# One contraction block of the third query/key piece moved ahead of the second memory rows, with a third staging buffer

## The chip, the cores and the metric

The kernel runs on one core of one Trainium2 chip. The metric is the device time of one execution in microseconds (us), lower is better. TensorE is called PE, its weight loads PEld, VectorE DVE, ScalarE ACT, GpSimd POOL. A ratio in the batches is the mean time of one kernel's fast runs over that of the kernel before in the same rounds, with the first round, in which the profile is taken, left out. So it is not quite the ratio of the medians and means that stand beside it, which keep that run. A "batch" is a set of kernels timed on one chip together with the kernel before.

## The reference, cut to what matters

Part A is a recurrent attention layer: 64 segments of 32 rows, each with 8 memory rows in front. The memory rows of a segment are the first 8 output rows of the segment before it. So every segment waits for the end of its predecessor. Part B, a gated MLP, follows and is not touched.

```python
for s in range(n_seg):                       # 64 segments
    xs = x[:, s*seg_len:(s+1)*seg_len, :]
    h = jnp.concatenate([mem, xs], axis=1)   # 8 memory rows + 32 rows, 512 wide
    q = jnp.einsum('btd,dhe->bhte', h, Wq)   # 32 heads x 128; k and v alike
    ...                                      # scores, softmax, p @ v
    o = jnp.einsum('bhte,hed->btd', o, Wo)
    mem = o[:, :M, :]                        # the next segment's memory rows
    outs.append(o[:, M:, :])
```

## The kernel before

The 512-wide contraction is cut into four blocks (dc = 0 to 3). Queries and keys of a segment come in five pieces, each with a PSUM bank: piece 0 queries of the first 16 heads, 1 keys of the same, 2 queries of the other 16, 3 and 4 their keys in two halves. A "set" is four matmuls, one in each 32-column strip of the array; a set that is "held" keeps the weights which the set before it loaded.

```python
QKP = ((0,0,8,0,0), (0,0,8,1,1), (1,0,8,0,6), (1,0,4,1,7), (1,4,4,1,2))  # half, first pair, pairs, q/k, bank
OB2 = 6                                   # bank of the second half of the output projection

def QK_evac(piece):                       # PSUM -> staging (ACT), staging -> QT or KT (DVE transpose)
    b, p0, np_, mi, bank = piece
    st_ = Tst[:, mi, 64*p0:64*(p0+np_)]   # two staging buffers: queries, keys
    ...

# one segment; the second half of the memory rows (dc 2, 3) comes by mem_out(s-1, 1)
QK(s, 0, 0)                               # piece 0, block 0: first memory rows
QK(s, 1, 0, last=2, held=True)
if s > 0: mem_out(s - 1, 1)               # ends in an ACT copy into hT
QK(s, 0, 1)
QK(s, 1, 1, last=2, held=True)
QK(s, 0, 2)                               # needs that ACT copy: PE waits here
QK(s, 0, 3)
QK_evac(QKP[0])
QK(s, 1, 3, last=2, held=True); QK(s, 1, 2, last=2)
QK_evac(QKP[1])
QK(s, 2, 2, first=2, last=0, held=True); QK(s, 2, 3, first=2, last=0)
QK(s, 2, 1, first=2, last=0);            QK(s, 2, 0, first=2, last=0)
QK_evac(QKP[2])
...                                       # pieces 3 and 4
S_half(s, 0)                              # scores of the first half: need pieces 0 and 1 transposed
```

The softmax here doesn't subtract the row's maximum and nothing guards it: scores larger than these inputs give would overflow.

## Time and profile before

| what | value |
|---|---|
| median | 852.48 us (852.42 to 853.62, 3 runs) |
| span of the profiled execution | 848.4 us (that run took 850.12 us) |
| segments, first to last copy of memory rows | 58.5 to 664.6 us |
| pitch of a segment, undisturbed | 9.72 us |

The pitch is worked out from the trace: the distance between the ends of two successive ACT copies of memory rows, as the mean of the third to twelfth smallest of the 62 distances. The smaller ones are segments in which nothing accidental happens. How the views are read, and their lines, stands in the prediction.

### The profile page before, as it was taken

The page shows a single profiled execution, that of the slowest core. Times are in us where ns is not written, and L with a number is a line of the kernel's source. Part 1 is how long each engine was busy: PE and PEld are TensorE (multiplying, and loading weights), DVE is VectorE, ACT ScalarE, POOL GpSimd, SP SyncE. Part 2 cuts the span into 40 slices and gives each one's busy share as a digit, 9 for nine tenths or more (in the row PEclk, how much of TensorE's full clock was granted, in tenths as well). Part 3 has the DMA queues.
Part 4 walks back from the last instruction along what each step waited for, and adds up shares of the span by engine and source line. Part 5 has one row for each costly group of instructions (what it writes and reads, how often), then busy time and mean ns, then how long its engine had stood idle before and what let it go on. Part 6 is the DMA issues. An engine that isn't in the chain of part 4 may idle for free.

```text
span 848.4 us, 46072 instructions
## 1 busy us (share of the span) xinstructions
PE 834.1 (98%) x22552; PEld 438.3 (52%) x19480; DVE 515.3 (61%) x1322; ACT 471.7 (56%) x1367; POOL 168.7 (20%) x425
## 2 busy tenths in 40 slices
PE   8889999999999999999999999999999999999998
PEld 8545555555545555555555555555555544444443
DVE  3456666676666666666766666666666664453443
ACT  3446666766667676667666666767666755300000
POOL 7312212121212122221222121122111232100000
PEclk9999999999999999999999999999999999999999
DMA  9972220222332221322222324242321690033001
GB/s 319 392 231 75 69 74 28 60 72 61 77 92 58 50 66 43 75 38 61 60 73 73 95 57 80 60 94 72 58 52 56 188 280 7 1 112 106 32 12 40
DMA packets 112920, 75.25 MB, mean 89 GB/s; under 512 B 70728, under 2 KB 98512, under 8 KB 112720
## 3 DMA queue, kind: packets, MB, share of 16 engines
q1 hardware_dynamic: 111504, 70.88, 30.2%
q8 instruction: 166, 2.72, 1.3%
q0 software_dynamic: 384, 1.05, 0.3%
q10 hardware_dynamic: 832, 0.33, 0.1%
q14 instruction: 34, 0.28, 0.1%
HBM read 39.46 MB, written 20.58 MB: 71 GB/s over the span
## 4 chain that ended last, share of the span: by engine, by line
PE 92%; SPq 5%; DMA 1%; issue 0%; DVE 0%; ACT 0%
PE f_ps L289 33%; PE f_ps L701 14%; PE f_ps L290 12%; PE f_ps L1172 11%; PE f_ps L751 3%; PE f_ps L666 3%; PE f_ps L1165 3%; PE f_ps L1248 3%; SPq L329 3%; PE f_ps L1129 3%; PE f_ps L498 2%; DMA f_arena<-in_A_Wo_dram 1%; SPq L825 1%; PE f_ps L595 1%; PE f_ps L615 1%; PE f_ps L672 1%
## 5 line engine op out<-in xcount | busy, mean ns | idle before, releaser
L289 PE MATMUL f_ps<-f_arena,f_hT 128*32 128x512 bf16 (+1 forms) x5632 | 359.7, 331 | 0.3
L289 PEld LDWEIGHTS f_ps<-f_arena,f_hT 128*32 128x32 bf16 x5632 | 133.1, 96 | 161.6 <-issue 69.8
L290 PE MATMUL f_ps<-f_arena,f_hT 128*32 128x512 bf16 (+1 forms) x2560 | 188.5, 315 | 0.0
L559 ACT ACTIVATE f_Tst<-f_ps 128x512 bf16<-128x512 f32 (+1 forms) x320 | 149.7, 510 | 57.6 <-PE f_ps L289 53.9
L701 PE MATMUL f_ps<-f_arena,f_cT 128*32 128x256 bf16 x4096 | 130.6, 274 | 0.9 <-DMA f_arena<-in_A_Wo_dram 0.6
L638 POOL TENSOR_TENSOR f_E_sb<-f_R_sb,f_E_sb 128x64 bf16<-128x64 f32 x128 | 57.0, 446 | 362.1 <-ACT f_R_sb L630 362.1
L567 DVE STREAM_TRANSPOSE f_QT<-f_Tst 128x256 uint32<-128x256 uint32 x128 | 57.1, 446 | 94.3 <-ACT f_Tst L559 94.3
L701 PEld LDWEIGHTS f_ps<-f_arena,f_cT 128*32 128x32 bf16 x4096 | 90.0, 94 | 37.1 <-ACT f_cT L686 23.2
L1172 PE MATMUL f_ps<-f_arena 128*128 128x512 bf16 x448 | 100.6, 379 | 0.0
L688 DVE TENSOR_SCALAR f_cT<-f_ps 128x160 bf16<-128x160 f32 x256 | 65.2, 318 | 35.2 <-PE f_ps L672 35.2
L713 ACT ACTIVATE f_part<-f_ps 128x256 bf16<-128x256 f32 x128 | 49.1, 383 | 57.7 <-PE f_ps L701 53.7
L658 DVE TENSOR_SCALAR f_V_sb<-f_ps 128x512 bf16<-128x512 f32 (+1 forms) x128 | 71.1, 555 | 13.6 <-PE f_ps L289 13.6
L686 ACT ACTIVATE f_cT<-f_ps 128x160 bf16<-128x160 f32 x256 | 57.1, 310 | 36.3 <-PE f_ps L672 36.3
L1172 PEld LDWEIGHTS f_ps<-f_arena 128*128 128x128 bf16 x448 | 43.8, 98 | 52.8
L567 DVE STREAM_TRANSPOSE f_KT<-f_Tst 128x128 uint32<-128x128 uint32 (+1 forms) x192 | 65.9, 356 | 2.8
L626 ACT ACTIVATE f_R_sb<-f_ps 128x160 f32<-128x160 f32 x128 | 38.9, 304 | 34.8 <-PE f_ps L290 34.8
L634 DVE TENSOR_TENSOR f_E_sb<-f_R_sb,f_E_sb 128x160 bf16<-128x160 f32 x128 | 41.7, 326 | 23.4 <-ACT f_R_sb L630 23.4
L1178 DVE TENSOR_TENSOR f_arena<-f_ps,f_arena 128x512 f32<-128x512 f32 x28 | 19.3, 690 | 54.4 <-PE f_ps L1172 52.4
L289 PE MATMUL f_ps<-f_arena,f_hTe 128*32 128x512 bf16 x640 | 48.8, 382 | 0.0
L608 ACT ACTIVATE f_E_sb<-f_ps 128x224 bf16<-128x224 f32 x128 | 45.9, 359 | 0.1
L751 PE MATMUL f_ps<-f_arena,f_cTx 128*32 128x512 bf16 x512 | 43.9, 379 | 0.5 <-issue 0.4
L630 ACT ACTIVATE f_R_sb<-f_R_sb 128x160 f32<-128x160 f32 x128 | 42.6, 332 | 2.0
(123 smaller groups left out, 1027.3 us busy)
## 6 DMA issues: line engine op xcount, KB each, us to landing
wT_d<-f_wst SPq DMA_DIRECT2D x32, 256.0 KB
f_arena<-wT_d SPq DMA_DIRECT2D x32, 256.0 KB
f_arena<-in_A_Wv_dram SPq DMA_DIRECT2D x4, 1024.0 KB
f_arena<-in_A_Wk_dram SPq DMA_DIRECT2D x4, 1024.0 KB
f_arena<-in_A_Wo_dram SPq DMA_DIRECT2D x4, 1024.0 KB
f_Vx<-vext_d SPq DMA_DIRECT2D x124, 32.0 KB
f_arena<-in_A_Wq_dram SPq DMA_DIRECT2D x3, 1024.0 KB
vext_d<-f_Vs SPq DMA_DIRECT2D x20, 128.0 KB
```

What stands on the lines that cost most here:

```text
L289: return e.matmul(out, lhsT=lhsT, rhs=rhs, start=start, stop=stop, skip_group_check=True, tile_position=pos)
L290: return e.add_instruction(mybir.InstMatmult(name=nc.get_next_instruction_name(), engine=mybir.EngineType.PE, ins=[e.lower_ap(rhs), e.lowe ...
L559: act(lambda e: e.activation(out=st_.rearrange("p (hp i r) -> p hp i r", i=32, r=2), in_=ps[:, bank, 0:64 * np_].rearrange("p (hp r i) -> ...
L567: dve(lambda e: e.transpose(out=dst, in_=src), reads=tok, writes=[(nm, b, k) for k in halves(b, p0, np_)])
L638: pool(lambda e: e.tensor_tensor(out=ev, in0=rv, in1=ev, op=ALU.mult), reads=[("R", b), ("Ex", b)], writes=[("Ex", b)])
L658: dve(lambda e: e.tensor_scalar(out=dst, in0=src, scalar1=VSC, scalar2=None, op0=ALU.mult), reads=[PB(bank)], writes=tok)
L686: act(lambda e: e.activation(out=dst, in_=src, func=ACT.Copy, scale=UNSC), reads=[PB(PVB[c])], writes=tok)
L688: dve(lambda e: e.tensor_scalar(out=dst, in0=src, scalar1=UNSC, scalar2=None, op0=ALU.mult), reads=[PB(PVB[c])], writes=tok)
L701: pe(lambda e, h=h, g=g, i=i, b=b, c=c: e.matmul(ps[32 * g:32 * g + 32, bank, 0:d1 - d0], lhsT=cTh[:, i, 8:40], rhs=w_o[:, h, d0:d1], star ...
L713: act(lambda e: e.activation(out=part[:, s % 8, d0:d1], in_=ps[:, bank, 0:d1 - d0], func=ACT.Copy), reads=[PB(bank)], writes=[("part", s % ...
L751: pe(lambda e, h=h, g=g, i=8 * qr + bg: e.matmul(ps[32 * g:32 * g + 32, WXB, :], lhsT=cTx[:, rb % 2, i, :], rhs=w_o[:, h, :], start=(i < 4 ...
L1172: pe(lambda e: e.matmul(ps[:, bank, 0:TB], lhsT=z2[:, sc, fb * 128:(fb + 1) * 128], rhs=wTb[tb % 2][:, :, sc, :], start=(sc == 0), stop=(s ...
```

## The change

Its intent: one more set that needs only the first memory rows (piece 2, block 1) runs while PE would wait for the second rows. Piece 2's evacuation gets staging of its own, so that it need not wait for the transpose of piece 0, which now comes later. The first segment's memory rows live in that third buffer until it is needed, and the output projection moves from bank 6, which is now used early, to bank 7.

```diff
-    Tst = sb("Tst", [128, 2, 512], BF)
+    Tst = sb("Tst", [128, 3, 512], BF)
...
-    m0 = sb("m0", [M, D], BF)
+    m0 = Tst[0:M, 1, :]
+    m0tok = [("T", 1, 0), ("T", 1, 1)]
...
-    OB2 = 6
+    OB2 = 7
...
-        st_ = Tst[:, mi, 64 * p0:64 * (p0 + np_)]
+        tb = 2 if mi else b
+        st_ = Tst[:, tb, 64 * p0:64 * (p0 + np_)]
...
         QK(s, 1, 1, last=2, held=True)
+        QK(s, 2, 1, first=1, last=0, held=True)
         QK(s, 0, 2)
...
-        QK(s, 2, 2, first=2, last=0, held=True)
-        QK(s, 2, 3, first=2, last=0)
-        QK(s, 2, 1, first=2, last=0)
-        QK(s, 2, 0, first=2, last=0)
+        QK(s, 2, 2, first=1, last=0, held=True)
+        QK(s, 2, 3, first=1, last=0)
+        QK(s, 2, 0, first=1, last=0)
```

More of the change, by code (lines that the diff above doesn't have):

```diff
@@ L338, in fast_path @@
     load_xe(2, 6)
-    sp(lambda e: e.dma_start(m0[:], A_mem0[0]), writes=["m0"])
+    sp(lambda e: e.dma_start(m0[:], A_mem0[0]), writes=m0tok)
     pool(lambda e: e.memset(onesrc[:], 1.0), writes=["onesrc"])
@@ L450, in mem0_transpose @@
                                             identity=ident[0:M, 0:M]),
-               reads=["m0", "ident"], writes=[PB(bank)])
+               reads=m0tok + ["ident"], writes=[PB(bank)])
         src = psb[:, bank, 0:DC * M].rearrange("p (dc c) -> p dc c", dc=DC)
@@ L556, in QK_evac @@
         b, p0, np_, mi, bank = piece
-        st_ = Tst[:, mi, 64 * p0:64 * (p0 + np_)]
-        tok = [("T", mi, k) for k in halves(b, p0, np_)]
+        tb = 2 if mi else b
+        st_ = Tst[:, tb, 64 * p0:64 * (p0 + np_)]
+        tok = [("T", tb, k) for k in halves(b, p0, np_)]
         act(lambda e: e.activation(out=st_.rearrange("p (hp i r) -> p hp i r", i=32, r=2),
```

## The prediction

> **What bounds the kernel now.** I read the page first: engine shares, slices, chain of work that ended last. Its lines on this:
>
> ```profile
> PE 834.1 (98%) x22552; PEld 438.3 (52%) x19480; DVE 515.3 (61%) x1322; ACT 471.7 (56%) x1367; POOL 168.7 (20%) x425
> ...
> PEclk9999999999999999999999999999999999999999
> ...
> PE 92%; SPq 5%; DMA 1%; issue 0%; DVE 0%; ACT 0%
> ```
>
> The reader is to see that the chain is the TensorE (PE) for 92% of the span at the full granted clock, and that VectorE (DVE) and ScalarE (ACT) have slack. So only time in which PE issues nothing can be won, unless matmuls are taken out, and this change takes out none. The stages, from the windows view (first columns: stretch, its length, PE busy):
>
> ```profile
> 0.00:48.50 48.50, 43.63 (x728) 33.61 (x696) 19.20 (x36) 18.93 (x37) 21.66 (x76) 1.00 0.99 355
> 48.50:664.60 616.10, 611.51 (x20696) 321.02 (x17688) 408.19 (x1123) 410.84 (x1251) 129.22 (x310) 1.00 0.27 67
> 664.60:848.40 183.80, 178.97 (x1140) 83.68 (x1096) 87.92 (x164) 41.98 (x81) 17.80 (x39) 0.99 0.30 90
> ```
>
> The middle stretch is the 64 recurrent segments, where the change sits. PE busy there is 99%, but a busy interval is a modelled duration (a 512-column matmul shows 0.39 us while the next set starts 0.22 us later), so the lost time must be read from the starts of matmuls. Next the waits view, of weight loads (PEld):
>
> ```profile
> PEld f_ps L289 <- issue: 69.8, 193, 0.4
> ...
> PEld f_ps L289 <- ACT f_hT L730: 24.0, 63, 0.4
> ```
>
> L730 is the ACT copy that brings the second half of the new memory rows into hT. It makes PE wait once in each of the 63 segments that have a predecessor: 24.0/63 = 0.38 us of weight-load idleness each time. That is not yet lost time: a set of four matmuls that keeps the weights of the set before ("held") leaves the load row idle about as long anyway. So the timelines of one segment, PE and then its weight loads:
>
> ```profile
> 409.23 0.39 PE L289 MATMUL f_ps<-f_arena,f_hT 128*32 128x512 bf16 x4
> 409.45 0.39 PE L290 MATMUL f_ps<-f_arena,f_hT 128*32 128x512 bf16 x4
> 409.69 0.61 PE L289 MATMUL f_ps<-f_arena,f_hT 128*32 128x512 bf16 x8
> 410.13 0.39 PE L290 MATMUL f_ps<-f_arena,f_hT 128*32 128x512 bf16 x4
> 410.35 0.39 PE L289 MATMUL f_ps<-f_arena,f_hT 128*32 128x512 bf16 x4
> ```
>
> ```profile
> 409.69 0.12 PEld L289 LDWEIGHTS f_ps<-f_arena,f_hT 128*32 128x32 bf16 x8 [0.38 <-ACT f_hT L730]
> 410.14 0.11 PEld L289 LDWEIGHTS f_ps<-f_arena,f_hT 128*32 128x32 bf16 x4 [0.33 <-issue]
> ```
>
> Here 409.45 is the last set that can run on the first memory rows (piece 1, contraction block 1), and 409.69 is the first that needs the second rows (piece 0, block 2). An undisturbed set takes 0.216 us (410.13 to 410.35; the 12 matmuls at 410.78 last until 411.43, 0.65/3). From 409.45 to 410.13 are three sets: undisturbed 3 x 0.216 = 0.648. The single starts read 409.446, 409.691, 409.919, 410.135: steps of 245, 228 and 216 ns, sum 689. So the stall costs 689 - 648 = 41 ns: 29 ns of waiting and 12 ns because, after a blocked load, loads and matmuls start together. The loads agree: idle 0.38 when blocked against 0.33 when nothing is waited for, 0.05 of difference. Over all 63 segments the same three steps exceed 648 ns by 41.1 ns on average, nearly identical each time.
>
> **What the Trainium skill says.** (1) "TensorE: Matmul & The Clock Gate", section "Wait — 56ns, not 53.3ns?": warm back-to-back matmuls of 512 columns start 215.7 ns apart. The trace agrees if four column tiles count as one: 216 ns per set. So a set moved elsewhere costs the same there. (2) The same page, "Step-by-step: what each phase is for": PE pulls weight loads ahead of matmuls in flight while matmuls stay in order. The trace agrees: loads at 411.54 serve matmuls at 411.65. So fewer loads save nothing where they are hidden, and a held set ahead of a blocked load covers it. (3) "Perfetto Trace Analysis", "Tensor Engine Instruction (MATMUL, LD_WEIGHTS)": the end of a matmul is estimated. Hence I use starts. (4) The same page, "Summary: the profiler window per engine type": semaphore propagation is hidden from the DVE and ACT windows. The trace prices it: the copy L730 (183 ns) ends at 409.645, the load starts at 409.691, 46 ns later; from the DVE copy L728 (end 408.686) to its load (408.734) it is 48 ns.
>
> **The change part by part.**
>
> *Moved set.* Piece 2 (queries, second half) runs its block 1 directly after piece 1's block 1, held, before the second rows are needed. The set in place: 409.446 + 0.216 = 409.662 start, next set due 409.878. The load for block 2 can go from 409.691 (signal plus latency, as now), 0.187 us early. The whole wait is covered: -41 ns x 63 = -2.6 us. The first segment has no wait and gains nothing. Later one set of piece 2 is gone, so the matmul count is unchanged.
>
> *Weight loads.* That set now uses loads already made: 4 fewer per segment, 256 in all. They were hidden under a 0.216 us set: 0 us.
>
> *Evacuation of pieces 0 and 1.* They now complete one set later against the rest of the PE stream: +0.216. The timelines of ACT and DVE in the same segment show what hangs on it:
>
> ```profile
> 410.36 1.08 ACT L559 ACTIVATE f_Tst<-f_ps 128x512 bf16<-128x512 f32 x2 [0.72 <-PE f_ps L289]
> 411.65 1.31 ACT L559 ACTIVATE f_Tst<-f_ps 128x512 bf16<-128x512 f32 x3 [0.21 <-PE f_ps L289]
> ```
>
> ```profile
> 410.99 0.45 DVE L567 STREAM_TRANSPOSE f_QT<-f_Tst 128x256 uint32<-128x256 uint32 x1 [0.82 <-ACT f_Tst L559]
> 411.48 0.45 DVE L567 STREAM_TRANSPOSE f_KT<-f_Tst 128x256 uint32<-128x256 uint32 x1
> ```
>
> In old PE time the evacuations become 410.58 to 411.66. The third one wants to start at 411.655. Two such evacuations follow each other at 493 ns (410.360, 410.853), so ACT can take it from 411.069 + 0.493 = 411.56: no delay, 0.09 spare. The second transpose ends at 411.92 now, so 412.14 then. The first score weight load (S of the first half) stands at 412.196 and needs that end plus 0.048: 412.19. It just fits; its matmul starts only at 412.303, a further 0.107 of cushion. Cost: 0, with nearly nothing spare at the load.
>
> *Staging.* With the old shared buffer the third evacuation would wait for the first transpose, 411.44 + 0.216 = 411.66, so some 0.02 to 0.05 late. The third buffer removes that; the key pieces' buffer is free at 412.14 plus propagation against an evacuation at 412.31. Cost 0. The first memory rows as an alias of it cost nothing: they are read before segment 0, whose third evacuation is the first to write there.
>
> *Output bank 6 to 7.* The second half of the output projection starts after the first half, which already needed all context evacuations, bank 7's included; its own evacuation is awaited by the memory-row matmuls anyway. 0 us.
>
> Sum: -2.6 us; 852.48 - 2.6 = 849.9 us, -0.3%.
>
> **The rivals.** *A wait takes the place of the one removed.* For: the second transpose reaches the score load with about 0.01 us to spare. Against: the matmuls behind have 0.107 more, and today's distance, 0.27 us, repeats in nearly every segment. If 20 to 40 ns came back there per segment, the time would be 850.7 to 852.4. *The whole 0.38 us is won.* For: the waits view says 24.0 us in all. That would be 828 us, faster by 2.8%. Against: the matmul starts show only 41 ns lost. *The third evacuation becomes the bound.* If ACT slipped, key evacuations and the exponential behind them would slip; the exponential ends just as its sums are due (loads released at 413.270, matmuls at 413.297 against 413.298 undisturbed), so every nanosecond would cost. A slip of 0.1 would give +6.3 us, net 856. Against: 0.09 spare on ACT, as worked out. *A lost gain downstream.* The last stage is PE at 97% of its stretch, so segments that end earlier should start it earlier.
>
> **Range and chances.** The mechanism is deterministic and small: full gain 849.9, half eaten 851.2; runs of the kernel before spread from 852.42 to 853.62, so the noise is comparable with the effect. I give 848.9 to 851.4 for 8 in 10. A change of 2% is 17 us, over six times all that this wait costs: faster 0.01, within 0.98, slower 0.01.
>
> **What would show it.** Right: the L730 waits of PEld vanish or no longer disturb starts, steps around them at 216 ns; held matmuls 2560 to 2816, loads 256 fewer; segment pitch about 0.04 shorter; score loads waiting for the transposes at most a few ns. Wrong: a new entry of PEld for the scores behind the DVE transposes in most segments, a later exponential, or longer waits for the memory rows themselves.

## More of the kernel before

One caution for later: the span times the lowest pitch leaves a remainder. Between the first and the last copy lie 606.1 us, and 62 x 9.721 are 602.7; the 3.4 us over are what I call off-pitch time.

## The result, and the profile after

The changed kernel took 847.96 us (847.65 to 849.66, 4 runs) against 853.05 us (852.42 to 854.00, 4 runs). The ratio is 0.9943 (0.9926 to 0.9961): same at 2%, with a gain of 5.1 us in the medians. That is below the predicted range and twice the predicted gain.

The timelines of one segment after the change, PE first, then its weight loads, answer to those of before:

```profile
410.21 0.39 PE L290 MATMUL f_ps<-f_arena,f_hT 128*32 128x512 bf16 x4
410.42 0.60 PE L291 MATMUL f_ps<-f_arena,f_hT 128*32 128x512 bf16 x8
410.85 0.60 PE L290 MATMUL f_ps<-f_arena,f_hT 128*32 128x512 bf16 x8
411.28 0.39 PE L291 MATMUL f_ps<-f_arena,f_hT 128*32 128x512 bf16 x4
```

```profile
410.67 0.29 PEld L290 LDWEIGHTS f_ps<-f_arena,f_hT 128*32 128x32 bf16 x8 [0.38 <-ACT f_hT L732]
```

Two held sets now follow each other (410.42, eight matmuls of L291). The first set on the second rows starts at 410.85: from 410.42 to 411.28 are four sets in 0.86 us, 0.215 each. The blocked load goes at 410.67, 0.18 us before its matmuls are due. By single starts, the three steps around the wait are 215, 215 and 216 ns (medians of the segments), against 247, 227 and 216 before. The pitch fell from 9.721 to 9.680 us, so by some 40 ns.

The waits view of weight loads after the change:

```profile
PEld f_ps L290 <- issue: 69.8, 193, 0.5
...
PEld f_ps L290 <- ACT f_hT L732: 24.3, 63, 0.7
...
PEld f_ps L703 <- issue: 2.9, 2, 2.7
```

The row of the removed wait has not moved (24.0 before, 24.3 now), although it costs nothing any more: it counts idleness of the load row, which a held set makes anyway. Only the starts of the matmuls told the two cases apart. The third line is new, and it is the key to the rest: PE stood for 2.7 us in the middle of a run of like instructions and waited for no semaphore. The PE timeline there:

```profile
52.43 0.28 PE L703 MATMUL f_ps<-f_arena,f_cT 128*32 128x256 bf16 x1
55.20 0.62 PE L703 MATMUL f_ps<-f_arena,f_cT 128*32 128x256 bf16 x16 [2.49 <-issue]
```

The DMA view of this stretch, 52.43 to 55.20 us (queue, kind: packets, MB, share):

```profile
q1 hardware_dynamic: 1441, 0.85, 100.5%
q8 instruction: 1, 0.02, 2.5%
```

Two lines, of q10 and q14, are left out. All 16 DMA engines were full of data transfers, and one transfer of the instruction queue q8 came in between. In the packed records it landed 1.36 us before PE went on. I looked at every gap of over 0.3 us within the segments that no semaphore ended: in nearly every trace most of them end 1.2 to 1.7 us after such a transfer landed (for instance 14 of 14 in one profile of the kernel before). I read them as late instruction fetches. The Trainium skill, "Runtime: NRT & Kernel Launch", section "Instruction fetch mechanics", says that an engine is refilled in blocks of 16 KiB, 256 instructions, through a DMA queue of its own. The count of that queue agrees; before, then after:

```profile
q8 instruction: 166, 2.72, 1.3%
```

```profile
q8 instruction: 165, 2.70, 1.3%
```

256 loads fewer, one block fewer.

A later count in the kept traces makes this reading firm. The 20 profiles have 192 gaps of this kind from 48.5 to 670 us (starts of matmuls over 0.3 us apart, no semaphore ending a wait). Before each of them I counted the matmuls and weight loads that PE had run, and divided by 256. In 176 of the 192 the remainder is 190 or 191, so these gaps stand at the same place of a block of 256 instructions. Of the other 16, 14 lie at 58 to 61 us, in the first segments, and two just behind another gap. These stalls differ from run to run. The profiled run of the kernel before happened to be its fastest and that of the changed kernel its slowest, so their spans differ by 0.5 us only (848.4 and 847.9) and hide the 2.6 us that the pitch shows.

### The profile page after: what moved, and what is told of

It reads as the page before. It is cut to its first block, busy times and chain, and to the rows that moved or that the text cites. A ratio compares the mean times of both kernels' runs of the same rounds, so it can differ in the third digit from the quotient of the medians.

```text
span 847.9 us, 45745 instructions
## 1 busy us (share of the span) xinstructions
PE 832.4 (98%) x22545; PEld 438.3 (52%) x19224; DVE 515.5 (61%) x1322; ACT 471.2 (56%) x1367; POOL 168.6 (20%) x425
## 4 chain that ended last, share of the span: by engine, by line
PE 92%; DMA 3%; SPq 3%; issue 1%; ACT 1%; DVE 0%; ACTq 0%
PE f_ps L290 31%; PE f_ps L703 14%; PE f_ps L291 13%; PE f_ps L1174 11%; PE f_ps L753 3%; PE f_ps L668 3%; PE f_ps L1167 3%; PE f_ps L1250 3%; PE f_ps L1131 2%; SPq L330 2%; PE f_ps L499 2%; DMA f_arena<-in_A_Wk_dram 2%; PE f_ps L597 1%; PE f_ps L617 1%; DMA f_arena<-in_B_w_in_dram 1%; PE f_ps L674 1%
## 5 line engine op out<-in xcount | busy, mean ns | idle before, releaser
L291 PE MATMUL f_ps<-f_arena,f_hT 128*32 128x512 bf16 (+1 forms) x2816 | 203.1, 321 | 0.0
```

Source lines behind the costliest of these rows:

```text
L291: return e.add_instruction(mybir.InstMatmult(name=nc.get_next_instruction_name(), engine=mybir.EngineType.PE, ins=[e.lower_ap(rhs), e.lowe ...
```

## The experiments

Theory 1: the covered wait (41 ns in 63 segments, 2.6 us) is the whole gain, and the rest of the 5.1 us is chance. Theory 2: something beside it gains as much again. Candidates were the staging, the bank, the shifted addresses, and the 256 weight loads saved.

### First batch: the parts apart

**The kernel before as a control.** No edit.

> The kernel before, unchanged, as a control of the comparison itself. Both theories expect a ratio of 1.000 within 0.001. If it lies 0.002 or more off 1, the measured 0.9943 of the change is partly a shift between runs and not of the kernel. Its profile is a second sample of the kernel before: steady segment pitch 9.72 us again.

Measured: ratio 1.0005 (0.9988 to 1.0023). The comparison is fair, but single runs of this unchanged kernel went from 851.0 to 855.3 us here. The three runs that I had seen spread over 1.2 us.

**The change again.** No edit.

> The changed kernel again, in more rounds. Theory 'the covered wait is all' (41 ns in 63 segments, 2.6 us): ratio 0.9970. Theory 'something beside it gains as much again': ratio 0.994 to 0.9945. The profile should show the pitch of 9.68 us in either case; where the second theory holds, the surplus must lie in segments off the pitch or outside the segments.

Measured: 0.9978 (0.9964 to 0.9993), pitch 9.679 us. This is nearer to theory 1 than the first result.

**The moved set alone**, from the kernel before:

```diff
         QK(s, 1, 1, last=2, held=True)
+        QK(s, 2, 1, first=1, last=0, held=True)
...
-        QK(s, 2, 2, first=2, last=0, held=True)
-        QK(s, 2, 3, first=2, last=0)
-        QK(s, 2, 1, first=2, last=0)
-        QK(s, 2, 0, first=2, last=0)
+        QK(s, 2, 2, first=1, last=0, held=True)
+        QK(s, 2, 3, first=1, last=0)
+        QK(s, 2, 0, first=1, last=0)
```

> Only the set of piece 2 is moved ahead; staging, first memory rows and output bank as before. Theory 'the covered wait is all': 0.9970, like the whole change, since the late third evacuation (some 0.03 us, by the shared staging buffer) lies in ACT slack. Theory 'staging is needed': less gain than the whole change, 0.998 or more, with a wait of the third evacuation for the first transpose. Theory 'the surplus comes with the move' : 0.994.

Measured: 0.9974 (0.9961 to 0.9988), pitch 9.679 us: as good as the whole change. The third staging buffer and the bank are not needed for the gain.

**The rest without the moved set**, from the changed kernel: the four lines of piece 2 go back to their old places, the other hunks of the change stay.

> The change without the moved set: third staging buffer, aliased first memory rows, output bank 7. Theory 'the covered wait is all': ratio 1.000, since none of these waits was on the path. Theory 'staging, bank or the moved addresses bring the surplus': 0.997 to 0.998.

Measured: 1.0008 (0.9992 to 1.0023), pitch 9.726 us as in the control. Staging, alias, bank and shifted addresses are worth nothing.

### Second batch: more and less cover, and the loads

**The change a third time.** No edit.

> The changed kernel a third time, to decide between 0.9943 of its first runs and 0.9978 of its second. Theory 'the covered wait is all, the rest is stalls of PE on late instruction fetches, which differ from run to run': 0.9960 to 0.9980. Theory 'a systematic surplus': 0.9950 or less.

Measured: 0.9957 (0.9935 to 0.9979), pitch 9.681 us: outside what either theory asked for, though the interval covers theory 1.

**The moved set loads its weights again**, so that PE has as many instructions as before the change:

```diff
-        QK(s, 2, 1, first=1, last=0, held=True)
+        QK(s, 2, 1, first=1, last=0)
```

> The whole change, but the moved set loads its weights again (not held), so PE has as many instructions as before (256 loads more than the change). Theory 'the covered wait is all': the same time as the change, ratio 0.997 to before, steady pitch 9.68 us. Theory 'fewer instructions mean fewer fetch stalls, and that is the surplus': 1 to 2 us slower than the change, with a larger sum of stalls that no semaphore ends.

Measured: 0.9978 (0.9958 to 0.9998), pitch 9.679 us. The mean was 851.9 us against 849.7 of the change, at the same pitch: 2.2 us slower (1.8 by the ratios), which is about what theory 2 asked for. The interval holds theory 1's 0.997 too, so this batch alone does not decide.

**One set less ahead of the wait**, from the kernel before:

```diff
-        QK(s, 1, 1, last=2, held=True)
         QK(s, 0, 2)
...
         QK(s, 1, 3, last=2, held=True)
+        QK(s, 1, 1, last=2)
         QK(s, 1, 2, last=2)
```

> From the kernel before, the opposite step: piece 1's block 1 goes behind the wait, so one set less covers it. If a set ahead of the wait is worth its 0.216 us until the wait is used up: wait 245 - 216 + 216, so 216 ns more in each of 63 segments, pitch 9.94 us, +13.6 us, ratio 1.0160. If the wait also moves up with the PE (a chain of its own that shrinks): clearly less, below 1.010.

Measured: 867.39 us, ratio 1.0159 (1.0136 to 1.0182), pitch 9.938 us: 217 ns more, as worked out. Its PE timeline (the first line has the wait in it, the second is an undisturbed run of as many matmuls):

```profile
410.05 1.08 PE L289 MATMUL f_ps<-f_arena,f_hT 128*32 128x512 bf16 x12
...
411.82 0.82 PE L289 MATMUL f_ps<-f_arena,f_hT 128*32 128x512 bf16 x12
```

Twelve matmuls take 0.26 us longer over the wait: 0.216 and the 0.04 of before. The rows arrive at a fixed time after the last segment's work; a set ahead of them is worth its full length until the wait is used up.

**One set more ahead of the wait**, from the changed kernel: piece 2's block 0 goes up too, held behind piece 1's block 0.

```diff
         QK(s, 1, 0, last=2, held=True)
+        QK(s, 2, 0, held=True)
...
-        QK(s, 2, 1, first=1, last=0, held=True)
+        QK(s, 2, 1, held=True)
...
-        QK(s, 2, 2, first=1, last=0, held=True)
-        QK(s, 2, 3, first=1, last=0)
-        QK(s, 2, 0, first=1, last=0)
+        QK(s, 2, 2, held=True)
+        QK(s, 2, 3)
...
-        QK(s, 3, 0, held=True)
+        QK(s, 3, 0)
```

> From the changed kernel, one set more ahead of the wait (piece 2's block 0 too). Theory 'the wait is already covered, and the score loads behind the transposes of pieces 0 and 1 are now the next limit': nothing gained, and a new wait of the score loads: transposes 216 ns later, 8 ns spare at the load and 105 ns of cushion from load to matmul leave 100 to 115 ns in 64 segments, pitch 9.78 to 9.80, +6.4 to +7.4 us over the change, ratio to before 1.0045 to 1.006. Theory 'more ahead is better still, or harmless': 0.997 or less.

Measured: 857.07 us, ratio 1.0048 (1.0027 to 1.0069), pitch 9.800 us, 120 ns over the change. The new wait of the score loads is in the waits view:

```profile
PEld f_ps L597 <- DVE f_KT L569: 14.2, 64, 0.7
```

In the changed kernel the transpose that releases these loads and the loads themselves stand like this (DVE, then PEld):

```profile
412.62 0.45 DVE L569 STREAM_TRANSPOSE f_KT<-f_Tst 128x256 uint32<-128x256 uint32 x1
```

```profile
413.13 0.27 PEld L597 LDWEIGHTS f_ps<-f_QT,f_KT 128*32 128x32 bf16 x16
```

The end at 413.07 and the start at 413.13 leave 0.06 us (median of the segments 56 ns, predicted 56), which is little more than the signal takes. With one set more, a new wait of 120 ns per segment comes up at the scores. Of these two choices the change is the right one.

### Third batch: chance or loads

**The change a fourth time, and the kernel before as a second control.**

> The changed kernel on one more chip session, beside three kernels that settle the surplus. Theory 'covered wait alone' : 0.9970 within the noise (0.0015); 'surplus by fewer instructions': 0.995 to 0.996.

> The kernel before as a second control: ratio 1.000 within 0.002, and another sample of how much time the stalls that no semaphore ends take in it.

Measured: 0.9964 (0.9943 to 0.9986) and 1.0001 (0.9976 to 1.0026). The first lies within theory 1's noise and just outside what theory 2 asked for, but its interval holds both. Single runs of the control went from 851.1 to 857.9 us.

**The moved set loading again, repeated.**

> The change with the moved set loading its weights again, repeated, since it was 2.1 us slower than the change in one session (849.7 against 851.9 us mean) at the same pitch. Theory 'chance': within 1 us of the change. Theory '256 loads more mean more fetch stalls': again about 2 us slower.

Measured: 0.9989 (0.9972 to 1.0007); mean 853.8 us against 851.5 of the change, 2.3 us slower (2.1 by the ratios), pitch 9.682 us. Chance is unlikely twice. The waits that no semaphore ends, in the output projection, from 48 to 720 us (changed kernel, then this one, same batch):

```profile
PEld f_ps L703 <- issue: 2.2, 3, 1.4
```

```profile
PEld f_ps L703 <- issue: 5.5, 6, 3.0
```

The two longest, 1.4 and 3.0 us, are those at 55 us, where the DMA engines are full. The same line reads 1.9 against 3.5 us in the second batch and 3.2 against 5.1 in the fourth; in three profiles of the kernel before it reads 0.6, 2.5 and 1.5. With one profile of each, this illustrates and does not prove.

**All five held sets of 512 columns load again**, 1280 loads over the change: `held=True` taken from QK(s, 1, 0), (s, 1, 1), (s, 2, 1), (s, 1, 3) and (s, 2, 2).

> The change with all five held sets of 512 columns loading their weights again: 1280 loads more than the change, all hidden under matmuls. Steady pitch 9.68 us under both theories. Theory 'fewer instructions are worth some 2 us per 256': about 10 us slower than the change, ratio to before 1.005 to 1.008. Theory 'instructions are not the cause': within 1 us of the change, 0.997 to 0.998.

Measured: 1.0016 (0.9998 to 1.0033), mean 855.7 us, 4.2 us slower than the change at the same pitch (9.679 us). The sign is that of theory 2, the size less than half of its forecast of 10: the loss does not grow in proportion.

### Fourth and fifth batch: number of instructions or weight loads

**The change a fifth time, and the reload a third time.**

> The changed kernel as the reference of this batch. Three batches gave differences of 2.2, 3.7 and 3.3 us to before: again 2 to 4 us, ratio 0.9955 to 0.9978.

> The change with the moved set loading again, a third time, to be compared with the split one in the same batch. Twice it was 2.2 us slower than the change: again 1.5 to 2.9 us. Theory 'chance': within 1 us.

Measured: 0.9971 (0.9954 to 0.9989), and 0.9983 (0.9962 to 1.0004) with one run at 859.1 us. The means differ by 2.0 us and the medians by 1.7, but the 859.1 is the profiled run: by the ratios, which leave it out, the difference is 1.0 us, below the forecast of 1.5 to 2.9.

**A held set run as two halves**: four matmuls more per segment, no load more.

```diff
-        QK(s, 1, 1, last=2, held=True)
+        QK(s, 1, 1, last=2, held=True, part2=0)
+        QK(s, 1, 1, last=2, held=True, part2=1)
```

Here `part2` picks one half of the set's columns in the weights and in the bank.

> The change with one held set of 512 columns (piece 1, block 1) run as two of 256: four matmuls more in each segment and no load more, so as many PE instructions as before the change. Theory 'the number of PE instructions counts, since stalls follow late fetches': like the variant that loads again, 2 us slower than the change. Theory 'the weight loads themselves cost something': like the change, within 0.5 us (two matmuls of 256 take 218 ns for 216).

Measured: 0.9986 (0.9969 to 1.0003), 0.9 us slower than the change in the mean (1.3 by the ratios, where the reload of this batch is 1.0 slower); the pitch of 9.684 us explains 0.2 of it. It lies between the theories and decides nothing.

**Another set made held**, from the changed kernel, in search of a faster version:

```diff
         V_half(s, 1, (0, 2), 0, 3, 0)
+        V_half(s, 1, (2, 4), 0, 3, 1, held=True)
         sm_norm(0)
...
-        V_half(s, 1, (2, 4), 0, 3, 1)
         V_half(s, 1, (2, 4), 1, 3, 1)
```

> The change and another set made held: the second half's value columns of block 0 follow their neighbour ahead of the sums, 256 loads fewer. Theory 'fewer PE instructions': 1 to 2 us faster than the change, if the later sums do not make the context products wait. If they do (evacuation of the values on ACT about 60 ns later, half of the segments with little spare): up to 3 us slower.

Measured: 1.0011 (0.9991 to 1.0031), 3.1 us slower than the change, pitch 9.746 us. PE's wait for the normalised weights of the context products rose from 1.6 us in 6 segments to this:

```profile
PEld f_ps L668 <- DVE f_E_sb L636: 10.8, 38, 0.4
```

The later sums cost more on the path than the loads could bring.

**Five sets reloaded, repeated, beside the same five sets run as halves.** The second has `part2=0` and `part2=1` for each of the five, and the second half of a piece's first set starts no new accumulation.

> The change with five held sets of 512 columns loading again (1280 PE instructions more), repeated as the reference for the split variant. It was 0.9 us slower than before and 4.2 us slower than the change: again 0 to 2 us slower than before, ratio 1.000 to 1.002.

> The change with the same five sets each run as two of 256 columns, still held: 1280 PE instructions more than the change and not one load more. The extra starts cost 2 to 4 ns each, 10 to 20 ns per segment, about 1 us by the pitch. Theory 'the number of PE instructions counts': like the variant that loads again or slower, ratio 1.000 to 1.003. Theory 'the loads themselves count': 0.9975 to 0.9985, the change plus its 1 us.

Measured: 0.9999 (0.9980 to 1.0017), a hair below its forecast, and 1.0030 (1.0007 to 1.0054), at the upper end of theory 1. Both have 1280 PE instructions over the change, and the instruction queue shows it for both alike, here for the halves:

```profile
q8 instruction: 170, 2.79, 1.4%
```

The halves have not one load more than the change and yet are as slow as the reloads or slower. Their pitch of 9.691 us explains 0.7 us (11 ns in 64 segments), while 1.0030 against the change's mean of 0.9963 is 5.7 us (across batches). Theory 2's 0.9975 to 0.9985 lies outside the interval. So this speaks for the number of PE instructions and against the weight load as such. It is one batch of six runs, without the change beside it, and the profile of the halves, taken in their fastest run (852.4 us), does not show the loss: its off-pitch time is 5.2 us, no more than the change's.

### What the batches say together

| kernel | ratios to before | pitch, us | off-pitch time in its profiles, us |
|---|---|---|---|
| before, or change without the moved set | 1.0005, 1.0001, 1.0008 | 9.72 to 9.73 | 3.4, 5.3, 8.2, 5.7 |
| change, or moved set alone | 0.9943, 0.9978, 0.9957, 0.9964, 0.9971; 0.9974 | 9.68 | 4.5, 4.7, 4.7, 6.3, 6.8; 6.0 |
| moved set loads again | 0.9978, 0.9989, 0.9983 | 9.68 | 6.2, 8.7, 10.0 |

The mean of the change's five ratios is 0.9963, some 3.2 us of 853, with a standard error of about 0.5 us. The pitch gives 2.6. The off-pitch times average 5.7, 5.5 and 8.3 us in the three rows. With the means of all profiles of the first two rows the pitch falls by 44 ns, which is 2.8 us, and the four later ratios of the change alone give 2.8 us. So within the accuracy of these runs the change keeps what the pitch gives, and the 5.1 us of the first runs was luck.

Where the off-pitch time lies can be estimated from the traces: I compared each step between matmuls with the median of the same step in the other segments, and added up the excess at the ends of the 256-instruction blocks alone. That gives 3.5 to 7.4 us in the four profiles of the first row, 4.1 to 6.3 in the six of the second and 6.3 to 9.4 in the three of the third, and in all 20 profiles it is within 1.7 us of the off-pitch time. The same sum taken half a block away gives 0.9 to 1.6 us in every profile, which is scatter of the method. So off-pitch time is, by this estimate, mostly waiting at the ends of blocks. The segments have 148 such ends before and with the reload, and 147 with the change, so the differences do not come from their number.

## Why the prediction was right or wrong

- **The wait, 41 ns in 63 segments: right.** The steps became 215 ns, the pitch fell by 40 ns in the first pair of profiles and by 44 in the mean of all, and one set less or more ahead gave the pitches worked out beforehand (9.938 against 9.94, 9.800 against 9.78 to 9.80).
- **Evacuations, staging, alias, bank, 0 us: right.** The parts without the moved set gave 1.0008, the moved set alone 0.9974. The distance from the transpose's end to the score load was 56 ns, as computed. The rival of a new wait there was a real danger, one set further on. Its sum holds a slip: 20 ns in 63 segments are 1.3 us, so its lower end is 851.2 us, not 850.7.
- **"The mechanism is deterministic and small", with noise "from 852.42 to 853.62" and a range from 848.9 to 851.4: the step that failed.** The covered wait is deterministic, the rest of the time is not. The prediction had no term for the waits at the ends of instruction blocks. The off-pitch time, mostly these by the estimate above, came to 3.4, 5.3 and 8.2 us in three profiles of the same unchanged kernel. Three timed runs over 1.2 us hid this: single runs of the unchanged kernel later went from 850.8 to 857.9 us, and the changed kernel's from 847.7 to 854.3. The first median of the change, 847.96 us, fell below the range by luck; the other four batches had medians of 849.6 to 851.2, all inside it. The five medians span 3.2 us; the range was 2.5 wide.
- **"Weight loads ... 0 us": incomplete, but not what the number missed by.** The loads are hidden for the array, as the steps at 215 ns show, but each is an instruction that PE must fetch (165 blocks against 166). With the moved set loading again the kernel was slower in three batches at an unchanged pitch: by 2.2, 2.3 and 2.0 us in the means, by 1.8, 2.1 and 1.0 in the ratios, about half of what the change gains. The halves point to the number of instructions, without settling it. Against the kernel before, a gain from the saved loads is not shown: the change gains 3.2 us with a standard error of 0.5, and the pitch alone gives 2.6 to 2.8.
- **What stays open.** The reload variant has the covered wait and before's instruction count, and gains 0.9 to 1.9 us by its ratios instead of 2.6. Its off-pitch time is larger than before's at an equal number of instructions. A part of its loss even lies behind the segments, where the kernels run the same instructions: from the last copy of memory rows to the end its three profiles show 185.1, 186.0 and 187.9 us, against 183.8 to 184.8 before and 183.9 to 185.1 with the change. It may be that a wait gives the fetch time to catch up and that covering it takes this away, or that the place of the 256-instruction blocks in the segment matters; no run separated these. That the excess does not grow in proportion (1 to 2 us for 256, 3 to 4 for 1280) fits neither simply.

## What to carry to other kernels

When an in-order engine waits for late data, fill the wait with work that needs only what is there, and take the loss from the starts of its instructions, not from an idle row: that row read 24 us before and after. Follow what the moved work delays, and count its margin in the same nanoseconds; here one set was free and a second cost 120 ns per segment. Where effects are a few tenths of a per cent, repeat the unchanged kernel first and read a steady pitch out of the trace, which resolved some 40 ns while the total times scattered by several us.

## What the Trainium skill lacked or had wrong

- "Runtime: NRT & Kernel Launch", "Instruction fetch mechanics", calls the cost of a 16 KiB block boundary mostly hidden. In this kernel of 42,000 PE instructions it was not always: 176 of 192 gaps that no semaphore ended stand at one place of a 256-instruction block, and almost all of them follow a landing of the instruction queue by 1.2 to 1.7 us. They reached 3.0 us at 55 us, while data filled the DMA engines, and about 1 us later, with these engines 27% busy. The estimate above puts the loss in the segments at 3.5 to 9.4 us. The block size agrees: 166 transfers before, 165 with 256 instructions fewer, and 170 with 1280 more than that.
- "TensorE: Matmul & The Clock Gate", "Step-by-step: what each phase is for", describes loads pulled ahead of matmuls, which the trace confirms; no page that I read adds what a hidden load still costs as a fetched instruction: loading one set again, 256 loads, cost 1.0 to 2.3 us here.
- No page that I read gives the refill after a blocked load: the set after it started 227 instead of 216 ns later in nearly every segment of the kernel before.
